# Gate visits merged, gate weights loaded into columns, two output tiles evicted in halves, and a new written order

## The chip, the cores and the metric

The kernel runs on one core of one Trainium2 chip. The metric is the device time of one execution in microseconds (us). The kernel before was timed three times: 266.11, 266.49 and 266.73, median 266.49.

## The reference, cut to what matters

The output is `g * a + (1 - g) * b` for 2048 tokens of 512 features in bf16. `a` is an attention with a memory over four segments of 512 tokens and 32 heads of 16 features; `b` is a GLU with 1792 hidden features; `g` is one gate for each token. Both branches read `A_x`.

```python
x = A_x
g = sigmoid((x * gate_w).sum(-1, keepdims=True))
q, k, v = x @ wq, x @ wk, x @ wv          # heads, 4 segments of 512
for s in range(4):
    logits = qs @ ks.T * 0.25 + mask      # keys after the query are masked
    a_dot = softmax(logits) @ vs
    a_mem = (phi(qs) @ M) / (phi(qs) @ z + 1e-6)
    o = gb * a_mem + (1 - gb) * a_dot     # gb = sigmoid(beta), one per head
    M = M + phi(ks).T @ vs;  z = z + sum(phi(ks))
a = o @ wo
b = (gelu(x @ w_gate) * (x @ w_up)) @ w_down
return g * a + (1 - g) * b
```

## The kernel before, in words

The program is a list of named tasks. A task is one or a few instructions on one engine. A long string `ORDER`, written out, lists all tasks; each engine runs its tasks in the order of that string, and a task that takes a new PSUM bank names it there behind a colon (`out3_1_0:0` takes bank 0). Four banks (`psD`) are shared by the dense matmuls, the weighted sums and the small products; one four-bank region (`psX`) takes the score fills, one at a time. Waits are derived from what tasks read and write, bank reuse included. So the string alone sets the order on each engine, and on SP's queue the order in which DMAs are issued; an instruction that waits holds up all behind it on its engine.

Names carry the segment first, then the tile. For segment `s`:

- `xtr0_n`, `xev0_n`: the first segment's x is loaded in four pieces (`ld_x0_hk`: token half h, feature half k), turned on TensorE by 16 transposes (L773) and copied out on VectorE or ScalarE (L781, L782). The x of later segments comes by DMA transposes `ld_xS_kb` (L331) into one of three buffers `xT`, so that segment 3 uses the buffer of segment 0.
- `K`, `Q`, `V`: projections in groups of four matmuls of 512 columns, emitted in pairs `a` and `b` (L452; the first two K tiles in halves of 256 columns, L477); `Kev`, `Qev`, `Vev` evict them on either engine, `kpada` and `kpadb` write masked copies of k (L488), and `phka`, `phkb`, `phkc` compute phi (L462 to L465; `phq...` for q).
- `vsh` (L503) are shifted copies of v, and `ktr` (L562) transposes of phi(k), both by DMA from SP.
- `mz` (L567): 64 small matmuls, the memory sums; `mzacc` adds them up on VectorE. `nz`, `nd`, `ndp`, with the transposes `tpS_z` and `tpS_m`, read the memory.
- `stS_tX` (L597): a fill of scores, t a quarter of the heads and X one of A to E; `exp` (L603) on ScalarE; `msk` (L609) on GpSimd; `pvS_t` (L640): 64 matmuls, the weighted sums, in eight blocks of keys, each waiting for its own mask; `tpS_dtj` (L520), `pvp` (L650, L651) and `ot` (L657 adds the memory part, L659 transposes into `oT`) follow on VectorE. `oT` is one buffer for all segments.
- `G`, `gelu` or `gd`, `U`, `h` (L689, VectorE): the two GLU products. `outS_q_p` (L702): the down product of output tile q in five pieces of 2 or 3 matmuls. `wev` (L707 on ScalarE, L710 on VectorE) scales it by 1 - g, called `omgt`; `wo` (L718) is the attention's output product; `oev` (L722, VectorE) adds `gtok` times it; `dma` (L725) stores the tile through one of two buffers `ost`. The last tile, 15, has `wo` and `oev` in two halves of 256 columns and two stores, from SP and ScalarE.
- `gate`, `gz`, `gr`, `go`: the token gates of one segment, each a visit of its own to a bank: 16 matmuls of one column of weights by 128 tokens (L421), a transpose and a clamp on VectorE (L428, L429), exp on ScalarE (L430), and `omgt`, `gtok` on VectorE (L432 to L434).

The gate weights are loaded by SP as four rows of 128 into a corner of `omem` (`ld_gw`), turned into four columns by a small matmul (`gwtr`, L744) and copied to `gatew` (`gwev`, L746). Large weights come in halves of 0.9 MB: `wg0`, `wg1`, `wu0`, `wu1`, `wd0`, `wd1`. The head of the string, where the loads and the start are laid out, reads:

```python
ld_wk10 ld_wq00 ld_wq01 ld_wq10 ld_wv ld_beta ld_gw ld_wg0 ld_wg1 ld_x1_2 ld_x1_1 ld_x1_0 ld_x1_3 xtr0_0:1 xtr0_1:2
xtr0_3:3 xtr0_2:0 xev0_3:a xev0_2:a causal vones0 xev0_0:d xev0_1:d K0_1a:1 K0_0a:2 K0_0b K0_1b K0_2a:3 K0_2b Kev0_2:d
```

Of the kernel before, what the change touches and what calls it, by code (L numbers as in the profile page):

```python
# [14 lines left out]
P = 128  # L15
# [220 lines left out]
def _build(es, nc, A_x, A_wq, A_wk, A_wv, A_wo, A_beta, B_w_gate, B_w_up, B_w_down, gate_w, out):  # L236
# [40 lines left out]
    gt = sb("gt", [P, P], F32)  # L277
# [31 lines left out]
    def bk(s):  # L309
        return ("bank", s)  # L310
# [12 lines left out]
    gw4, ball = omem[0:4, 0, 0:P], omem[:, 1, 0:H]  # L323
# [21 lines left out]
    ld_w("gw", SP, gw4, gate_w.rearrange("(kb p) -> kb p", p=P), [("gw4",)], 0.01, ["x0_10"])  # L345
# [68 lines left out]
    def gates(s):  # L414
        sl = Slot()
        c = slice(4 * s, 4 * s + 4)

        mm = []
        for kb in range(4):
            for i in range(4):  # L420
                mm.append(I(lambda e, i=i, kb=kb: e.matmul(  # L421
                    BK[sl.i][32 * i:32 * i + 1, 0:128], gatew[:, kb:kb + 1],
                    xT[s % R_XT][:, kb, :].rearrange("p (q j r) -> p j q r", j=4, r=32)[:, i],
                    start=(kb == 0), stop=(kb == 3), tile_position=(0, 32 * i)),
                    [*x_of(s % R_XT, kb), ("gatew",)], [bk(sl)]))
        one(f"gate{s}", PE, 0.26, mm)
        one(f"gz{s}", DVE, 0.36, [
            I(lambda e: e.transpose(gt[:, :], BK[sl.i][:, 0:128]), [bk(sl)], [("gt",)]),  # L428
            I(lambda e: e.tensor_scalar(gz[:, c], gt[:, 0:128:32], ZMAX, None, ALU.min), [("gt",)], [("gz", s)])])  # L429
        one(f"gr{s}", ACT, 0.2, [I(lambda e: e.activation(gr[:, c], gz[:, c], ACTF.Exp), [("gz", s)], [("gr", s)])])  # L430
        one(f"go{s}", DVE, 1.2, [
            I(lambda e: e.tensor_scalar(gr1[:, c], gr[:, c], 1.0, None, ALU.add), [("gr", s)], [("gr1", s)]),  # L432
            I(lambda e: e.reciprocal(omgt[:, c], gr1[:, c]), [("gr1", s)], [("omgt", s)]),
            I(lambda e: e.tensor_tensor(gtok[:, c], gr[:, c], omgt[:, c], ALU.mult), [("gr", s), ("omgt", s)],  # L434
              [("gtok", s)]),
        ])
# [32 lines left out]
    def project(s):  # L469
# [36 lines left out]
        gates(s)  # L506
# [50 lines left out]
    def memory_write(s):  # L557
# [3 lines left out]
        for t in range(4):  # L561
# [4 lines left out]
        sl = Slot()  # L566
        one(f"mz{s}", PE, 0.45, [I(lambda e, c=c, kt=kt, g=g, sl=sl: e.matmul(  # L567
# [10 lines left out]
                [("mzacc",), ("gphm",)], [("mzq",)])])  # L578
        one(f"zq{s}", POOL, 0.25, [I(lambda e: e.tensor_tensor(
# [112 lines left out]
    def outputs(s):  # L692
        for qt in range(4):
# [4 lines left out]
            for pi, (a, z) in enumerate(((0, 3), (3, 6), (6, 8), (8, 11), (11, 14))):  # L698
                mm = []
                for fb in range(a, z):  # L700
# [8 lines left out]
                    [bk(sl), ("omgt", s)], [("wds", wi)])]),  # L709
                (DVE, 0.66, [I(lambda e, sl=sl, gt=gt, wi=wi: e.tensor_scalar(  # L710
                    wds[wi][:, :], BK[sl.i][:, :], omgt[:, gt:gt + 1], None, ALU.mult),
                    [bk(sl), ("omgt", s)], [("wds", wi)])])], L_DVE)
            last = gt == 4 * NSEG - 1
            parts = (slice(0, 256), slice(256, 512)) if last else (slice(0, 512),)
            ko = [[("ost", oi, 0)], [("ost", oi, 1)]] if last else [[("ost", oi, 0), ("ost", oi, 1)]]
            for ci, c in enumerate(parts):
                so = Slot()
                one(f"wo{s}_{qt}_{ci}", PE, 4 * T_MM / len(parts), [I(lambda e, kb=kb, q=q, so=so, c=c: e.matmul(  # L718
                    BK[so.i][:, c], oT[:, kb, q], wo[:, kb, c], start=(kb == 0), stop=(kb == 3)),
                    [("oT", kb), ("wo", kb, 0), *([("wo", kb, 1)] if kb < 3 else [])], [bk(so)]) for kb in range(4)])  # L720
                one(f"oev{s}_{qt}_{ci}", DVE, 0.66 / len(parts) + 0.03, [I(
                    lambda e, so=so, gt=gt, wi=wi, oi=oi, c=c: e.scalar_tensor_tensor(  # L722
                        out=ost[oi][:, c], in0=BK[so.i][:, c], scalar=gtok[:, gt:gt + 1], in1=wds[wi][:, c],
                        op0=ALU.mult, op1=ALU.add), [bk(so), ("gtok", s), ("wds", wi)], ko[ci])])
                one(f"dma{gt}_{ci}", (SP, ACT)[ci], 0.5, [I(lambda e, gt=gt, oi=oi, c=c: e.dma_start(  # L725
                    out[0, gt * 128:(gt + 1) * 128, c], ost[oi][:, c]), ko[ci], [("out", gt, ci)],
                    dma_sem=sem(f"s_out{gt}_{ci}"))], lat=2.0)
                outs.append(f"s_out{gt}_{ci}")
# [3 lines left out]
    def head_gates():  # L732
# [3 lines left out]
        for c in range(4):  # L736
            for m0, m1, h in ((2 * c, 8, 8 * c), (0, 2 * c, 8 * c + 8 - 2 * c)):
                if m0 < m1:
# [4 lines left out]
        sg = Slot()  # L743
        one("gwtr", PE, T_TR, [I(lambda e: e.transpose(BKbf[sg.i][:, 0:4], gw4, ident[0:4, 0:4]),  # L744
                                 [("gw4",), ("omem", 0), ("ident",)], [bk(sg)])])
        one("gwev", DVE, 0.1, [I(lambda e: e.tensor_copy(gatew[:, :], BKbf[sg.i][:, 0:4]), [bk(sg)], [("gatew",)])])  # L746
# [39 lines left out]
    for s in range(NSEG):  # L786
        if s == NSEG - 1:
            ld_xt(s)
# [63 lines left out]
ld_wk10 ld_wq00 ld_wq01 ld_wq10 ld_wv ld_beta ld_gw ld_wg0 ld_wg1 ld_x1_2 ld_x1_1 ld_x1_0 ld_x1_3 xtr0_0:1 xtr0_1:2  # L852
xtr0_3:3 xtr0_2:0 xev0_3:a xev0_2:a causal vones0 xev0_0:d xev0_1:d K0_1a:1 K0_0a:2 K0_0b K0_1b K0_2a:3 K0_2b Kev0_2:d
Kev0_0:a Kev0_1:a kpadb0_1 phka0_0 K0_3a:0 K0_3b Q0_1a:2 Q0_0a:1 Q0_0b Kev0_3:a phkb0_0 kpada0_0 kpada0_1 phka0_2
kpada0_2 kpadb0_2 kpadb0_0 kpada0_3 kpadb0_3 Q0_2a:3 Q0_2b Qev0_0:a Qev0_2:a Q0_1b Qev0_1:a Q0_3a:0 Q0_3b Qev0_3:a
V0_2a:1 gwtr:3 V0_1a:2 gwev st0_0A:0 gate0:0 phkc0_0 gz0 V0_1b V0_0a:3 V0_0b V0_3a:0 V0_3b exp0_0A phkb0_2 st0_0B:0
exp0_0B Vev0_0:d Vev0_1:d Vev0_3:d V0_2b G0_2a:3 G0_3a:2 G0_3b G0_1a:0 st0_0C:0 Gev0_3:d betab G0_2b G0_1b G0_0a:2
G0_0b Vev0_2:a exp0_0C Q1_3a:1 Gev0_1:d Gev0_0:a st0_0D:0 V1_3a:0 V1_3b Q1_2a:2 Q1_2b Q1_3b phkc0_2 Vev1_3:d Qev1_2:d
Qev1_3:d exp0_0D bexp Gev0_2:a st0_0E:0 exp0_0E gr0 gate1:0 G0_6a:2 G0_6b K1_1a:3 V1_0a:1 K1_1b vsh0_20 vsh0_00
vsh0_01 vsh0_21 ld_wu1 Gev0_6:d Kev1_1:d gz1 st0_1A:0 exp0_1A G1_6a:2 V1_0b G1_6b msk0_0C msk0_0B msk0_0D msk0_0A  # L860
msk0_0E pv0_0:30 st0_1B:0 Gev1_6:a tp0_d00:0 Vev1_0:a exp0_1B G0_4a:2 G0_4b gq Gev0_4:d tp0_d01:1 pvp0_01 K1_3a:1
K1_3b Kev1_3:a K1_2a:3 st0_1C:0 exp0_1C Q1_1a:2 K1_0a:0 K1_0b G0_5a:1 G0_5b st0_1D:0 exp0_1D ld_wo00 ld_wo10 ld_wo30
ld_x2_1 ktr0_1 ktr0_3 ld_wo11 ktr0_2 ld_x2_2 ld_wo01 ld_wu0 ktr0_0 ld_wd0 ld_wo21 ld_x2_0 ld_x2_3 ld_wd1 Kev1_0:d
Gev0_5:d pvp0_00 Q1_1b G1_1a:0 K1_2b V1_1a:1 V1_1b Kev1_2:d ot0_0 Vev1_1:d Qev1_1:d st0_2A:0 exp0_2A msk0_1A msk0_1D
msk0_1C msk0_1B G0_10a:3 G1_1b G0_10b Gev1_1:d gph kpada1_3 go0 gd0_10 G1_13a:1 G1_13b G0_8a:2 G0_8b G1_7a:0 G1_7b
gd1_13 gd1_7 G0_13a:3 G0_13b gd0_13 gd0_8 G0_9a:1 G0_9b gd0_9 G1_9a:0 G1_9b gd1_9 gelu0 st0_2B:0 pv0_1:32 kpadb1_3
tp0_d11:2 tp0_d10:1 kpadb1_0 G0_7a:1 G0_12a:0 G0_12b gd0_12 G1_8a:2 G0_7b G0_11a:3 G0_11b gd0_7 gd0_11 G1_8b gd1_8
U0_4a:0 Q1_0a:1 U0_4b U0_9a:3 kpada1_2 pvp0_10 kpadb1_2 pvp0_11 h0_4 phka1_2 U0_9b U0_3a:2 h0_9 U0_3b U0_8a:0 Q1_0b
phka1_0 Qev1_0:d U0_8b h0_8 exp0_2B st0_2C:0 phkb1_2 exp0_2C mz0:3 U0_5a:1 U0_1a:0 U0_1b U0_5b st0_2D:0 h0_3 mzacc0
h0_1 h0_5 phqa1_0 G1_3a:2 U0_11a:3 V1_2a:0 U0_11b h0_11 V1_2b Vev1_2:d kpadb1_1 exp0_2D st0_2E:0 G1_3b U0_6a:1 G1_5a:3  # L870
G1_5b U0_6b exp0_2E Gev1_5:a phqa1_2 Gev1_3:d h0_6 phkc1_2 st0_3A:0 G1_2a:0 U0_7a:2 G1_2b msk0_2B msk0_2C msk0_2D
msk0_2A exp0_3A msk0_2E pv0_2:31 phqb1_0 Gev1_2:d tp0_d21:0 tp0_d20:1 st0_3B:0 U0_7b U0_12a:0 G1_4a:1 U0_12b G1_4b
h0_7 h0_12 exp0_3B st0_3C:0 exp0_3C U0_13a:3 G1_0a:2 U0_13b G1_0b U0_10a:0 st0_3D:0 pvp0_20 kpada1_0 Gev1_4:d h0_13
kpada1_1 Gev1_0:d U0_10b U0_2a:1 U0_0a:3 h0_10 U0_2b h0_2 U0_0b K2_1a:2 h0_0 phqb1_2 exp0_3D phkb1_0 st1_0A:0 K2_3a:0
K2_1b K2_3b msk0_3A msk0_3B msk0_3C msk0_3D exp1_0A pv0_3:13 phkc1_0 st1_0B:0 Kev2_1:a Kev2_3:a exp1_0B K2_2a:2 K2_2b
Kev2_2:a tp0_d30:2 tp0_d31:1 K2_0a:0 G1_11a:1 K2_0b ld_x3_3 ld_wo20 ktr1_2 vsh1_00 ktr1_0 ktr1_1 vsh1_20 vsh1_01
vsh1_21 ktr1_3 st1_0D:0 gr1 exp1_0D Q2_3a:3 Q2_3b out0_0_0:2 out0_0_1 st1_0E:0 Qev2_3:d pvp0_21 Kev2_0:a exp1_0E
V2_3a:3 out0_1_0:0 V2_3b out0_1_1 Vev2_3:a st1_0C:0 exp1_0C msk1_0E zq0 msk1_0B msk1_0C msk1_0D msk1_0A out0_0_2
out0_1_2 G1_11b out0_1_3 out0_1_4 out0_0_3 ot0_1 pvp0_30 phqc1_0 pvp0_31 ot0_2 out0_0_4 Q2_1a:3 st1_1A:0 Q2_1b ot0_3
wev0_0:d wev0_1:d wo0_1_0:2 out0_3_0:0 out0_3_1 out0_3_2 Qev2_1:d kpada2_1 oev0_1_0 phqc1_2 out0_3_3 out0_3_4 pv1_0:32  # L880
tp1_d01:0 tp1_d00:2 gd1_11 gelu1 exp1_1A st1_1B:0 exp1_1B out0_2_0:1 out0_2_1 wo0_0_0:2 st1_1C:0 out0_2_2 G2_4a:3
# [77 lines left out]
```

## Time and profile before

| what | value |
|---|---|
| three timed runs | 266.11, 266.49, 266.73 us |
| profiled execution, first to last instruction (its span) | 266.5 us |
| what lies around the span | nothing that the times show: the span is the median |
| TensorE matmuls | 2816, busy 261.3 us |
| VectorE, ScalarE, GpSimd busy | 204.8, 207.2, 96.2 us |
| granted TensorE clock (mean) | 1.000 |
| DMA | 14.92 MB, 56 GB/s in the mean |

Busy time of TensorE counts overlapping matmuls once, and the ends of matmuls are modelled; what one matmul costs is read from start to start. LDWEIGHTS run beside the matmuls. A wait is put down to the semaphore that came last.

### The profile page before, as it was taken

The page shows a single profiled execution, that of the slowest core. Times are in us where ns is not written, and L with a number is a line of the kernel's source. Part 1 is how long each engine was busy: PE and PEld are TensorE (multiplying, and loading weights), DVE is VectorE, ACT ScalarE, POOL GpSimd, SP SyncE. Part 2 cuts the span into 40 slices and gives each one's busy share as a digit, 9 for nine tenths or more (in the row PEclk, how much of TensorE's full clock was granted, in tenths as well). Part 3 has the DMA queues.
Part 4 walks back from the last instruction along what each step waited for, and adds up shares of the span by engine and source line. Part 5 has one row for each costly group of instructions (what it writes and reads, how often), then busy time and mean ns, then how long its engine had stood idle before and what let it go on. Part 6 is the DMA issues. An engine that isn't in the chain of part 4 may idle for free.

```text
span 266.5 us, 6614 instructions
## 1 busy us (share of the span) xinstructions
PE 261.3 (98%) x2816; PEld 112.4 (42%) x2816; DVE 204.8 (77%) x389; ACT 207.2 (78%) x170; POOL 96.2 (36%) x160
## 2 busy tenths in 40 slices
PE   6999999999999999999999999999999999999995
PEld 2634444443443443444444443444344444434442
DVE  1466578578976669998797998897987797968975
ACT  1589888988899988989988979749798967477601
POOL 6003705036430816042254538423635035072600
PEclk9999999999999999999999999999999999999999
DMA  6993339950025120000004100011001000010002
GB/s 195 264 214 53 149 75 156 235 158 0 2 48 109 23 59 22 2 0 4 20 2 64 39 2 2 20 42 39 4 15 52 2 0 2 2 59 2 20 2 79
DMA packets 25251, 14.92 MB, mean 56 GB/s; under 512 B 14086, under 2 KB 24198, under 8 KB 25222
## 3 DMA queue, kind: packets, MB, share of 16 engines
q1 hardware_dynamic: 23990, 13.91, 22.3%
q10 hardware_dynamic: 1232, 0.59, 0.8%
q8 instruction: 22, 0.36, 0.5%
q14 instruction: 7, 0.06, 0.1%
HBM read 8.14 MB, written 2.10 MB: 38 GB/s over the span
## 4 chain that ended last, share of the span: by engine, by line
PE 97%; DMA 2%; issue 0%; DVE 0%; SPq 0%; DVEq 0%
PE psD L452 54%; PE psD L702 19%; PE psX L597 9%; PE psD L640 7%; PE psD L718 5%; DMA pt<-in_A_x_dram 2%; PE psD L477 1%; PE psD L773 1%; PE psD L567 1%; PE psD L421 0%; PE psX L545 0%; PE psD L535 0%; DVE ost L722 0%; SPq L327 0%; DVEq L806 0%
## 5 line engine op out<-in xcount | busy, mean ns | idle before, releaser
L603 ACT ACTIVATE pt<-psX 128x2048 bf16<-128x2048 f32 x72 | 135.1, 1876 | 32.3 <-PE psX L597 31.6
L609 POOL TENSOR_TENSOR pt<-pt,ctri 128x256 bf16<-128x256 bf16 x128 | 90.9, 717 | 153.9 <-ACT pt L603 149.4
L452 PE MATMUL psD<-xT,wu 128*128 128x512 bf16 x224 | 58.0, 380 | 0.0
L452 PE MATMUL psD<-xT,wg 128*128 128x512 bf16 x224 | 56.4, 380 | 0.0
L702 PE MATMUL psD<-wd,gb 128*128 128x512 bf16 x224 | 54.4, 380 | 0.0
L689 DVE TENSOR_TENSOR gb<-psD,gb 128x512 bf16<-128x512 f32 x56 | 37.5, 683 | 11.9 <-PE psD L452 11.5
L520 DVE STREAM_TRANSPOSE tT<-psD 128x512 f32<-128x512 f32 x35 | 23.4, 695 | 11.3 <-PE psD L640 11.1
L702 PEld LDWEIGHTS psD<-wd,gb 128*128 128x128 bf16 x224 | 20.7, 98 | 25.8 <-issue 2.8
L452 PEld LDWEIGHTS psD<-xT,wg 128*128 128x128 bf16 x224 | 20.3, 98 | 26.2 <-issue 2.8
L452 PEld LDWEIGHTS psD<-xT,wu 128*128 128x128 bf16 x224 | 20.1, 98 | 25.6 <-issue 3.7
L597 PE MATMUL psX<-qT,kD 32*128 32x192 bf16 (+7 forms) x512 | 28.6, 287 | 0.0
L597 PEld LDWEIGHTS psX<-qT,kD 32*128 32x128 bf16 x512 | 8.2, 92 | 25.9 <-ACT pt L603 19.5
L651 DVE SCALAR_TENSOR_TENSOR ob<-tT,gq,rc 128x256 bf16<-128x256 f32 x32 | 18.2, 570 | 1.1
L640 PE MATMUL psD<-pt,vnat 64*17 64x128 bf16 (+7 forms) x512 | 18.7, 283 | 0.0
L445 DVE CAST gb<-psD 128x512 bf16<-128x512 f32 x23 | 15.7, 684 | 3.7 <-PE psD L452 3.6
L640 PE MATMUL psD<-pt,vsh 64*17 64x128 bf16 (+7 forms) x512 | 18.3, 283 | 0.0
L452 PE MATMUL psD<-wv,xT 128*128 128x512 bf16 x64 | 18.0, 381 | 0.0
L452 PE MATMUL psD<-xT,wq 128*128 128x512 bf16 x64 | 17.0, 380 | 0.0
L718 PE MATMUL psD<-wo,oT 128*128 128x512 bf16 (+1 forms) x68 | 16.2, 367 | 0.0
L640 PEld LDWEIGHTS psD<-pt,vnat 64*17 64x17 bf16 x512 | 11.6, 86 | 8.7 <-issue 3.8
L680 ACT ACTIVATE gb<-psD 128x512 bf16<-128x512 f32 x28 | 14.7, 602 | 0.3 <-PE psD L452 0.3
L452 PE MATMUL psD<-xT,wk 128*128 128x512 bf16 x56 | 14.6, 380 | 0.0
(96 smaller groups left out, 250.4 us busy)
## 6 DMA issues: line engine op xcount, KB each, us to landing
out_dram<-ost SPq DMA_DIRECT2D x15, 128.0 KB, 1.7
wg<-in_B_w_gate_dram SPq DMA_DIRECT2D x2, 896.0 KB, 6.9
wu<-in_B_w_up_dram SPq DMA_DIRECT2D x2, 896.0 KB, 5.4
wd<-in_B_w_down_dram SPq DMA_DIRECT2D x2, 896.0 KB, 7.3
vsh<-vnat SPq DMA_DIRECT2D x16, 68.0 KB, 2.1
wq<-in_A_wq_dram SPq DMA_DIRECT2D x4, 128.0 KB, 4.8
wv<-in_A_wv_dram SPq DMA_DIRECT2D x1, 512.0 KB, 4.7
pt<-in_A_x_dram SPq DMA_DIRECT2D x2, 128.0 KB, 3.5
```

Of the source, the lines that this page charges most:

```text
L445: (DVE, 0.60, [I(lambda e: e.tensor_copy(dst, src()), [bk(sl), *reads], writes)]),
L452: one(f"{name}{'abcd'[h // 2]}", PE, 2 * T_MM, [I(lambda e, i=i: e.matmul(BK[sl.i][:, :], lhs(i), rhs(i), start=(i == 0), stop=(i == n - 1 ...
L520: one(f"tp{name}", DVE, 0.605, [I(lambda e, ts=ts, bank=bank: e.transpose(tT[ts.i][:, :], bank()), [key], [("tT", ts)])])
L597: ins.append(I(lambda e, c=c, kb=kb, ncol=ncol, c0=c0, g=g: e.matmul(XALL[:, g * 512 + c0:g * 512 + c0 + ncol], kD[b][quad(g), c, kb, :], ...
L603: one(f"exp{s}_{name}", ACT, 2048 * 0.000833 + 0.05, [I(lambda e: e.activation(pt[slot][:, :, :], xin, ACTF.Exp, scale=ATT_SCALE), [("X", ...
L609: ins.append(I(lambda e, mv=mv: e.tensor_tensor(mv, mv, cm, ALU.mult), [("pt", slot), ("causal",)], [("pt", slot)]))
L640: ins.append(I(lambda e, kb=kb, slot=slot, c0=c0, n=n, g=g, c=c, r0=r0, sl=banks[j], va=va: e.matmul(BK[sl.i][32 * c:32 * c + 17, 64 * kb: ...
L651: I(lambda e, ts=ts, t=t, j=j, dst=dst: e.scalar_tensor_tensor(out=dst, in0=t_rows(ts, 16), scalar=gq[:, 2 * t + j:2 * t + j + 1], in1=rc_ ...
L680: one(f"gd{s}_{ft}", ACT, 0.485, [I(lambda e, gi=gi, f=f, sl=sl: e.activation(gb[gi][:, f, :], BK[sl.i][:, :], ACTF.Gelu_apprx_tanh), [bk( ...
L689: one(f"h{s}_{ft}", DVE, 0.605, [I(lambda e, sl=sl, gi=gi, f=f: e.tensor_tensor(gb[gi][:, f, :], BK[sl.i][:, :], gb[gi][:, f, :], ALU.mult ...
L702: mm.append(I(lambda e, fb=fb, gi=gi, f=f, q=q, sl=sl: e.matmul(BK[sl.i][:, :], gb[gi][:, f, q], wd[:, fb, :], start=(fb == 0), stop=(fb = ...
L718: one(f"wo{s}_{qt}_{ci}", PE, 4 * T_MM / len(parts), [I(lambda e, kb=kb, q=q, so=so, c=c: e.matmul(BK[so.i][:, c], oT[:, kb, q], wo[:, kb, ...
```

## The change

Five things change.

1. The gates of segments 0 and 1, and of 2 and 3, are computed together: 32 matmuls into the upper half (columns 256 to 511) of the bank that the memory sums `mz0` and `mz1` use, just ahead of them. `gz`, `gr` and `go` then run once for two segments, on twice the columns.
2. The gate weights are loaded by one DMA straight into four columns of `gatew`; `gwtr` and `gwev` go.
3. Tile 14 has `wo` and `oev` in halves like tile 15, but is still stored by one DMA, from SP.
4. The loads of segment 3's x are declared with segment 1 instead of segment 3.
5. The whole string `ORDER` is written anew.

The core of the diff:

```diff
-    ld_w("gw", SP, gw4, gate_w.rearrange("(kb p) -> kb p", p=P), [("gw4",)], 0.01, ["x0_10"])
+    load("gw", SP, lambda e: e.dma_start(gatew[:, :], gate_w.rearrange("(kb p) -> p kb", p=P),
+                                         allow_slow_non_contiguous=True), [("gatew",)], wait=[("ld", "x0_10")])
...
+    def gate_products(h, sl):
+        one(f"gate{h}", PE, 0.5, [I(lambda e, i=i, kb=kb, s=s: e.matmul(
+            BK[sl.i][32 * i:32 * i + 1, 256 + 128 * (s % 2):384 + 128 * (s % 2)], gatew[:, kb:kb + 1],
+            xT[s % R_XT][:, kb, :].rearrange("p (q j r) -> p j q r", j=4, r=32)[:, i],
+            start=(kb == 0), stop=(kb == 3), tile_position=(0, 32 * i)),
+            [*x_of(s % R_XT, kb), ("ld", "gw")], [bk(sl)])
+            for s in (2 * h, 2 * h + 1) for kb in range(4) for i in range(4)])
+
+    def gates(h, sl):
+        c = slice(8 * h, 8 * h + 8)
+        one(f"gz{h}", DVE, 0.5, [
+            I(lambda e: e.transpose(gt[:, :], BK[sl.i][:, 256:512]), [bk(sl)], [("gt",)]),
+            I(lambda e: e.tensor_scalar(gz[:, c], gt[:, 0:256:32], ZMAX, None, ALU.min), [("gt",)], [("gz", h)])])
...
         sl = Slot()
+        if s < 2:
+            gate_products(s, sl)
         one(f"mz{s}", PE, 0.45, [I(lambda e, c=c, kt=kt, g=g, sl=sl: e.matmul(
...
+        if s < 2:
+            gates(s, sl)
...
+            split = gt >= 4 * NSEG - 2
             last = gt == 4 * NSEG - 1
-            parts = (slice(0, 256), slice(256, 512)) if last else (slice(0, 512),)
+            parts = (slice(0, 256), slice(256, 512)) if split else (slice(0, 512),)
...
+                if last or ci == len(parts) - 1:
+                    kd, d = (ko[ci], c) if last else ([k for kk in ko for k in kk], slice(0, 512))
+                    one(f"dma{gt}_{ci}", (SP, ACT)[last and ci], 0.5, [I(lambda e, gt=gt, oi=oi, d=d: e.dma_start(
...
-        one("gwtr", PE, T_TR, [I(lambda e: e.transpose(BKbf[sg.i][:, 0:4], gw4, ident[0:4, 0:4]),
-                                 [("gw4",), ("omem", 0), ("ident",)], [bk(sg)])])
-        one("gwev", DVE, 0.1, [I(lambda e: e.tensor_copy(gatew[:, :], BKbf[sg.i][:, 0:4]), [bk(sg)], [("gatew",)])])
...
-        if s == NSEG - 1:
-            ld_xt(s)
+        if s == 1:
+            ld_xt(3)
```

Of the new order, the start (TensorE's tasks and SP's loads), one stretch with the second gate visit, and the end:

```python
ld_wk10 ld_wq00 ld_wq01 ld_wq10 ld_wv ld_beta ld_wg0 ld_gw ld_x1_2 ld_wg1 ld_x1_0 xtr0_2:0 xtr0_0:1 xtr0_1:2 xtr0_3:3
xev0_3:a vones0 xev0_0:d xev0_1:d K0_1a:1 xev0_2:a K0_0a:2 K0_1b K0_2a:3 K0_2b causal K0_0b Kev0_2:d Kev0_1:a kpadb0_1
...
oev0_2_0 pvp1_10 Gev2_6:a gate1:2 h1_0 kpadb2_0 mz1 V2_0a:0 V2_0b G2_13a:1 msk1_2A gelu2 gz1 U1_3a:3 Vev2_0:d U1_3b
...
U3_9a:1 ot3_0 st3_3C:0 exp3_3C h3_4 oev2_3_0 U3_9b out3_0_0:3 h3_9 out3_0_1 out3_0_2 st3_3D:0 out3_0_3 out3_0_4
out3_1_1 pvp3_20 exp3_3D ot3_1 out3_1_2 dma10_0 msk3_3A msk3_3B wev3_0:a msk3_3C pvp3_21 ot3_2 out3_1_3 msk3_3D
pv3_3:31 out3_2_0:2 tp3_d31:2 tp3_d30:0 out3_2_1 pvp3_31 out3_1_4 out3_2_2 pvp3_30 out3_3_0:1 out3_3_1 dma11_0
wev3_1:a ot3_3 wo3_1_0:0 wo3_0_0:3 out3_2_3 out3_3_2 oev3_0_0 out3_2_4 oev3_1_0 out3_3_3 out3_3_4 wev3_2:d wo3_2_0:3
wev3_3:a dma12_0 wo3_2_1:2 wo3_3_0:0 oev3_2_0 dma13_0 oev3_2_1 dma14_1 oev3_3_0 wo3_3_1:3 dma15_0 oev3_3_1 dma15_1
```

In the old string the end reads:

```python
msk3_2A msk3_2C msk3_2D msk3_2E pv3_2:21 h3_7 h3_4 tp3_d21:1 tp3_d20:0 pvp3_11 exp3_3A st3_3B:0 wo2_3_0:3 out3_1_0:0
...
U3_9a:1 exp3_3B st3_3C:0 U3_9b out3_0_0:2 out3_0_1 out3_0_2 exp3_3C st3_3D:0 exp3_3D msk3_3B msk3_3A msk3_3C msk3_3D
oev2_3_0 ot3_0 h3_9 pvp3_20 pvp3_21 ot3_1 ot3_2 out3_0_3 out3_1_1 out3_1_2 out3_0_4 out3_1_3 out3_1_4 pv3_3:31
tp3_d31:2 tp3_d30:0 pvp3_31 pvp3_30 ot3_3 wev3_1:d wev3_0:a dma10_0 dma11_0 out3_2_0:2 out3_2_1 out3_3_0:1 out3_2_2
out3_2_3 out3_2_4 out3_3_1 wo3_0_0:3 wo3_1_0:0 out3_3_2 oev3_0_0 oev3_1_0 dma12_0 dma13_0 out3_3_3 out3_3_4 wo3_2_0:3
wev3_2:a wev3_3:d wo3_3_0:0 wo3_3_1:2 oev3_2_0 oev3_3_0 oev3_3_1 dma14_0 dma15_0 dma15_1
```

SP's loads after `wv` and `beta` come in this order before: `gw`, `wg0`, `wg1`, `x1_2`, `x1_1`, `x1_0`, `x1_3`, four `vsh0`, `wu1`; afterwards: `wg0`, `gw`, `x1_2`, `wg1`, `x1_0`, `x1_1`, `wu1`, `x1_3`, three `vsh0`. On TensorE, `Q1_3a` comes four pairs of G matmuls behind `st0_0C` before, and directly behind it afterwards. `wd1` moves from behind the x2 loads to behind `ktr1_1`.

## The prediction

> **What bounds the kernel now.** I read the page's busy shares first, then the chain that ended last, then TensorE's own waits, and then the order of time at the two ends.
>
> ```profile
> PE 261.3 (98%) x2816; PEld 112.4 (42%) x2816; DVE 204.8 (77%) x389; ACT 207.2 (78%) x170; POOL 96.2 (36%) x160
> ...
> PE 97%; DMA 2%; issue 0%; DVE 0%; SPq 0%; DVEq 0%
> ```
>
> 97% of the chain is TensorE. Its own waits (the waits view for PE alone) are two, both in the first 6 us:
>
> ```profile
> PE psD L773 <- DMA pt<-in_A_x_dram: 1.4, 1, 1.4
> PE psD L369 <- POOL warm L365: 1.1, 1, 1.1
> ```
>
> From 5.65 to about 263.7 us TensorE never stands. So the time is the first useful matmul, plus the sum of TensorE's slots (start of one group to start of the next), plus the tail behind the last matmul. An edit counts only if it takes a slot away, moves an end, or opens a hole. One stretch of the timeline gives the prices:
>
> ```profile
> 15.11 0.59 PE L452 MATMUL psD<-wv,xT 128*128 128x512 bf16 x2
> 15.63 0.17 PE L744 MATMUL psD<-ident,omem 4*128 4x4 bf16 x1
> 15.74 0.61 PE L452 MATMUL psD<-wv,xT 128*128 128x512 bf16 x2
> 16.28 0.40 PE L597 MATMUL psX<-qT,kD 32*128 32x512 bf16 x4
> 16.60 0.39 PE L421 MATMUL psD<-xT,gatew 128*1 128x128 bf16 x16
> 16.93 2.33 PE L452 MATMUL psD<-wv,xT 128*128 128x512 bf16 x10
> ```
>
> A dense 512-column matmul takes 0.216. From dense into a group of another shape costs 0.10 more (15.11 to 15.63 is 0.53 for two). A score fill or a gate visit takes 0.33 in all, of which a gate visit is four rounds of 0.055 and 0.11 of leaving. The two timed ends are 266.11 and 266.73, the median 266.49, and the profiled span 266.5; so nothing measurable lies around the span and the sum is made against 266.5. A measurement of this kernel can tell about 0.2%, 0.53 us, from no change.
>
> **Gates.** The four visits take 0.326, 0.326, 0.342 and 0.327, together 1.32. Afterwards there are two visits of eight rounds, 2 x 0.44 = 0.88, directly followed by the memory sums. Before, mz1 directly followed by gate2 has a slot of 0.536, while mz0 and mz2, followed by dense work, have 0.639 and 0.597; so these two shapes change over without the 0.10, and mz1 gets its leaving cost back (+0.10). Saved: 1.32 - 0.88 - 0.10 = 0.34. If the change-over costs 0.10 after all, 0.14; if mz1 pays nothing, 0.44. The VectorE and ScalarE work of the gates (ten VectorE instructions fewer) is hidden: no slot waits for it, and omgt is first read by the output stage, some 15 us later.
>
> **Gate weights.** The transpose at L744 goes: 0.10 into it and 0.105 for it, 0.20 saved, with a VectorE copy of 0.16 beside it. The load becomes 512 elements of 2 bytes. The nearest row is the beta load, 128 runs of 64 bytes, which landed 0.19 after the wv load ahead of it in the queue; four times that is 0.8, and 0 is the other end; I take 0.3. Nobody waits for gatew until gate0, near 56 us. What it delays is queued behind it on SP: the x1 transposes.
> [...]
>
> **Head.** What is loaded first decides the start.
>
> ```profile
> 1.07 3.17 PE L369 MATMUL psD<-warm 128*128 128x512 bf16 x7 [1.07 <-POOL warm L365]
> 5.65 1.89 PE L773 MATMUL psD<-ident,pt 128*128 128x128 bf16 x16 [1.41 <-DMA pt<-in_A_x_dram]
> 7.33 2.76 PE L477 MATMUL psD<-xT,wk 128*128 128x256 bf16 x16
> 9.93 1.89 PE L452 MATMUL psD<-xT,wk 128*128 128x512 bf16 x8
> ```
>
> TensorE starts with xtr0_0, whose data (x0_00) landed at 5.60 in the trace's landing records; x0_10 landed at 3.44. Afterwards xtr0_2, on x0_10, comes first: it fills 4.03 to 4.46, and only three transposes of 0.427 stand behind 5.65. K0 starts at 6.93, not 7.33. But in the trace 256-column matmuls come every 0.213 until 9.04 and every 0.109 from there. If that step stays at 9.06, the 0.43 gained is slow time worth half, 0.21. Ends: 0.43 if the step moves along, 0 if an eviction intervenes. Walking VectorE and ScalarE through the new order (evictions 0.61 to 0.69, masked key copies 0.26 start to start) brings Qev0_2, the last input of the first fill, to 15.8; TensorE needs it at 16.3.
>
> **x1 and the SP queue.** Q1_3b now wants x1_3 at 22.4 (before, its first reader is V1_3b at 25.1), and the queue ahead of x1_3 has become wg0, gw, x1_2, wg1, x1_0, x1_1, wu1. In the trace wg0 and wg1 together took 6.0 from wv's landing and an x1 transpose 0.5. Three weights, four transposes and gw: 10.6 + 9.0 + 2.0 + 0.3 = 21.9; with the 2.5 that wd1 took behind a transpose, 20.4. I take no wait; the margin is the rival below. wd1, moved from 50.9 to behind ktr1_1 at about 79.4, lands at 84.2 by wu1's 4.8; out0_1_2 needs it at 86.1. The x3 loads move ahead of the second segment's vsh copies, and wait for xT[0] to be read out at 74.5; the copies are wanted at 95.
>
> **VectorE's queue.** ot (L657, L659) overwrites oT and so waits for the previous segment's last wo. The new order puts ot3_0 ahead of h3_4, and wo2_3_0 behind out3_1_0. From the start of st3_3B: wo2_3_0 ends at 1.84, seen 0.2 later; transpose 0.71 and h3_4 0.68 less 0.08 overlap give 3.36; out3_0_0, which reuses h3_4's bank, would start at 3.13. A hole of 0.29, bounds 0 to 0.5. Behind ot3_0 stand h3_4, oev2_3_0 and h3_9. The same sum for ot1_1 ahead of h1_8 (K3_1a waits) gives 0.15, for ot2_1 ahead of h2_2 (pv2_3) 0.05; as sums this fine err by 0.1, I take 0.10 for the two.
>
> **Tail.**
>
> ```profile
> 254.29 1.31 DVE L520 STREAM_TRANSPOSE tT<-psD 128x512 f32<-128x512 f32 x2 [1.32 <-PE psD L640]
> ...
> 257.44 0.71 DVE L659 STREAM_TRANSPOSE oT<-ob 128x512 bf16<-128x512 bf16 x1
> ...
> 258.40 1.89 PE L718 MATMUL psD<-wo,oT 128*128 128x512 bf16 x8
> ...
> 262.92 1.53 DVE L722 SCALAR_TENSOR_TENSOR ost<-psD,gtok,wds 128x512 bf16<-128x512 f32 x3
> 264.48 0.36 ACTq L725 DMA_DIRECT2D out_dram<-ost  x1
> ```
>
> pv3_3 ends at 254.07; VectorE has oT at 258.15, 4.08 later, and 20 dense matmuls (4.32) cover that. The new order has 17 there (3.67), so wo3_1_0 waits 0.46. Behind it on TensorE stands everything to the end. Against that, four half evictions replace one whole and two halves: from the start of wo3_2 the last one ends at 2.42 (last matmul issued 1.75, 0.20 to be seen, 0.47) instead of 2.60. Together +0.46 - 0.18 = +0.28; pv3_3 coming three matmuls earlier is only moved work. The output of tile 14 still leaves whole, after both halves.
> pv3_3 also follows its last fill by 3.45 instead of 4.10. The masks are done 3.88 after the fill, and pv reads that block 0.57 in, so 0.15 remains: no hole. It also waits for wev3_0 on ScalarE now (bank 3), done 2.9 after the fill. The other short distances (3.87) have more. Between two fills the new order keeps at least 2.37 on TensorE, as the old one did (fill to exp 0.45, exp 1.88, 0.055 to be seen).
>
> **Sum.** -0.34 - 0.20 - 0.21 + 0.28 + 0.29 + 0.10 = -0.08; all other slots are the same tasks, with as many entries from dense work. 266.4, with 266.0 to 267.0 as this case's own range.
>
> **Rivals.** *The holes do not open* (0.27): VectorE runs ahead of my sums and the head's 0.43 counts whole: -0.34 - 0.20 - 0.43 + 0.28 = -0.69, 265.8; without the tail's wait 265.4. For: the trace before has no hole, so the order was laid out with care. Against: ot's wait for wo is a fact of the new order.
> *The clock steps earlier* (0.05): xtr0_2 makes the stretch before 5.65 busier (from 4.03 it ran to 4.46 of it). If full speed came at 5.65, three transposes of 0.22 would end at 6.3, VectorE's copies at 6.9, and K0_1b, which needs ScalarE's second copy at about 7.7, at 8.3 instead of 9.3: 265.4. The step before is 3.41 after 5.65. [...]
> *x1_3 comes late* (0.28): in the trace its first part landed at 18.82 and its last at 20.50, 1.7 later. Such a straggler on the 21.9 gives 23.6, 1.2 past Q1_3b's need at 22.4, and TensorE stands for all of it: 267.6; with half of it 267.0 to 267.2. It decides once x1_3 lands after 22.4. Against it: wd1's faster row.
> *It does not do what it says*: no shared change-over costs +0.20 and stays within no change; it is in the first case.
>
> **Numbers.** The likeliest, 0.40: 266.4. Faster 0.32, slower 0.28. From 265.3 to 267.6 the range holds the rivals' prices and leaves out later stragglers and several gains at once.
>
> **What would show it.** Two gate slots of 0.44 just ahead of the memory sums, and no transpose of the gate weights. K0 at 6.9. No wait of PE on the xT transposes near 22; if there is one, the third rival. Holes of 0.3 at out3_0_0 (about 246) and of 0.5 ahead of the first wo behind the last weighted sum. The forecast is wrong in kind if PE's waits sum to over 1.5 us behind 6 us, or if the L477 matmuls run fast from the start.

## The result and the profile after

The changed kernel takes 268.55 us (median of four runs, 267.97 to 269.37), the kernel before 266.42 beside it: ratio 1.0077, 95% interval 1.0064 to 1.0091. It is slower by 2.1 us. The forecast was 266.4, with a range up to 267.6.

The page of the changed kernel, its busy line and its chain:

```profile
PE 256.1 (96%) x2782; PEld 112.3 (42%) x2819; DVE 203.0 (76%) x379; ACT 207.4 (78%) x168; POOL 96.4 (36%) x160
...
PE 80%; DVE 7%; DMA 6%; issue 3%; SPq 2%; ACT 0%; ACTq 0%
```

The chain was 97% TensorE; now VectorE and DMA have 13% of it. (37 of the 2819 matmul records are missing in this profile, which leaves seeming gaps called "issue"; the profile of c_after below has all records and no such gap among TensorE's waits.) The waits view for TensorE alone, columns: line and who released it, sum, number, longest in us:

```profile
PE psD L450 <- DMA xT<-in_A_x_dram: 1.1, 1, 1.1
...
PE psD L450 <- DVE gb L690: 0.4, 1, 0.4
...
PE psD L641 <- DVE vnat L443: 0.3, 1, 0.3
PE psX L598 <- DVE kD L486: 0.3, 1, 0.3
```

Before, both waits lay in the first 6 us. Now one on x1 and several behind VectorE lie in the middle. Slot by slot (start of a group to start of the next, minus the same slot in a gapless run) the holes are: 1.32 at Q1_3b, where x1_3 landed at 22.29 and TensorE stood ready for it at 21.0; and six behind VectorE, at 40 us (0.20, G1_13a waits for Vev1_1), 75.6 (0.33, st1_0A for kpada1_0), 76.2 (0.28, K2_3a for h0_10, next in VectorE's queue), 142.9 (0.41, pv1_3 for Vev2_1), 156 (0.30 inside pv2_0, h2_7) and 195 (0.27 inside pv2_3, h2_2). The six make 1.8. The timeline at the second and third of them (start, duration, engine, line, in brackets the idle time before and its releaser; the first matmul of K2_3a, at 76.23, is among the missing records, so that its row shows 0.43 and not 0.28):

```profile
74.75 1.42 POOL L610 TENSOR_TENSOR pt<-pt,ctri 128x256 bf16<-128x256 bf16 x2 [0.71 <-ACT pt L604]
...
74.79 0.78 DVE L486 TENSOR_SCALAR kD<-kT,maskA 128x512 bf16<-128x512 bf16 x1
...
75.63 0.39 PE L598 MATMUL psX<-qT,kD 32*128 32x512 bf16 x4 [0.27 <-DVE kD L486]
...
76.46 0.38 PE L450 MATMUL psD<-xT,wk 128*128 128x512 bf16 x1 [0.43 <-DVE gb L690]
```

The masked key copy kpada1_0 (L486) takes 0.78 here, and 0.35 where nothing disturbs it. It began 0.04 behind a GpSimd mask. The view shows no wait for it: the time appears as its own duration. TensorE's wait behind it does show.

Two things went as planned. The gate visits take 0.44 each, directly ahead of the memory sums, as a second execution of the changed kernel (c_after below) shows without a missing record:

```profile
55.63 0.62 PE L416 MATMUL psD<-xT,gatew 128*1 128x128 bf16 x32
...
56.07 0.71 PE L566 MATMUL psD<-vnat,phkt 128*32 128x34 bf16 x64
...
56.72 0.60 PE L450 MATMUL psD<-xT,wu 128*128 128x512 bf16 x2
```

And from the start of TensorE's last group (`wo3_3_1`) to the end of the span it is 3.21 us, against 3.38 in the profile before.

### The profile page after: what moved, and what is told of

It reads as the page before. It is cut to its first block, busy times and chain, and to the rows that moved or that the text cites. A ratio compares the mean times of both kernels' runs of the same rounds, so it can differ in the third digit from the quotient of the medians.

```text
span 267.6 us, 6577 instructions
## 1 busy us (share of the span) xinstructions
PE 256.1 (96%) x2782; PEld 112.3 (42%) x2819; DVE 203.0 (76%) x379; ACT 207.4 (78%) x168; POOL 96.4 (36%) x160
## 4 chain that ended last, share of the span: by engine, by line
PE 80%; DVE 7%; DMA 6%; issue 3%; SPq 2%; ACT 0%; ACTq 0%
PE psD L450 43%; PE psD L703 17%; PE psX L598 7%; PE psD L641 6%; PE psD L720 5%; DMA xT<-in_A_x_dram 2%; DMA wv<-in_A_wv_dram 2%; SPq L331 1%; DMA pt<-in_A_x_dram 1%; DVE gb L690 1%; DVE ob L652 1%; DVE kD L486 1%; DVE tT L517 1%; PE psD L566 1%; DVE ost L724 1%
## 5 line engine op out<-in xcount | busy, mean ns | idle before, releaser
L450 PE MATMUL psD<-xT,wu 128*128 128x512 bf16 x213 | 54.6, 379 | 1.8 <-issue 1.8
L450 PE MATMUL psD<-xT,wg 128*128 128x512 bf16 x216 | 54.3, 380 | 1.0 <-issue 0.8
L703 PE MATMUL psD<-wd,gb 128*128 128x512 bf16 x214 | 52.5, 380 | 1.5 <-issue 1.3
L703 PEld LDWEIGHTS psD<-wd,gb 128*128 128x128 bf16 x224 | 20.1, 98 | 25.9 <-issue 3.8
L724 DVE SCALAR_TENSOR_TENSOR ost<-psD,gtok,wds 128x512 bf16<-128x512 f32 (+1 forms) x18 | 12.1, 683 | 9.3 <-PE psD L720 9.3
L641 PE MATMUL psD<-pt,vsh 64*17 64x320 bf16 (+7 forms) x512 | 18.2, 283 | 0.0
L652 DVE SCALAR_TENSOR_TENSOR ob<-tT,gq,rc 128x256 bf16<-128x256 f32 x32 | 16.6, 520 | 1.1
L450 PE MATMUL psD<-wv,xT 128*128 128x512 bf16 x62 | 16.9, 380 | 0.3 <-issue 0.3
L443 DVE CAST gb<-psD 128x512 bf16<-128x512 f32 x20 | 13.4, 682 | 3.4 <-PE psD L450 3.3
```

Source lines behind the costliest of these rows:

```text
L450: one(f"{name}{'abcd'[h // 2]}", PE, 2 * T_MM, [I(lambda e, i=i: e.matmul(BK[sl.i][:, :], lhs(i), rhs(i), start=(i == 0), stop=(i == n - 1 ...
L641: ins.append(I(lambda e, kb=kb, slot=slot, c0=c0, n=n, g=g, c=c, r0=r0, sl=banks[j], va=va: e.matmul(BK[sl.i][32 * c:32 * c + 17, 64 * kb: ...
L652: I(lambda e, ts=ts, t=t, j=j, dst=dst: e.scalar_tensor_tensor(out=dst, in0=t_rows(ts, 16), scalar=gq[:, 2 * t + j:2 * t + j + 1], in1=rc_ ...
L703: mm.append(I(lambda e, fb=fb, gi=gi, f=f, q=q, sl=sl: e.matmul(BK[sl.i][:, :], gb[gi][:, f, q], wd[:, fb, :], start=(fb == 0), stop=(fb = ...
```

## Experiments

Ratios are to the kernel before, run beside the kernel on the same chip. VectorE's copies have line L486 in the changed kernel and those made from it, L488 in the kernel before.

**c_before, the kernel before again.**

> The kernel before once more, unchanged, as a control. Theory A: the profile before (span 266.5) caught an execution whose second piece of x, x0_00, landed late (5.60 against 4.77 in the profile after), and some 1.75 us lie around the span in every execution, as they do in the four executions of the changed kernel (269.37 against a span of 267.6, and three more with the same difference); then the spans of ordinary executions here are about 264.7 and the times 266.4. Rival: the span is the time, as the prediction said; then the spans are about 266.4.

266.44 (266.14 to 266.66), ratio 1.000 (0.9991 to 1.0009); the profiled execution took 266.56 with a span of 264.8, and in all ten the time is 1.7 to 1.8 above the span. Theory A. So the profile the prediction was made on (span 266.5) was not a usual execution: x0_00 landed at 5.60 there and at 4.69 here, and TensorE's 256-column matmuls ran at 0.109 from 6.9 on instead of 9.04. Two errors of 1.7 us, that execution and "nothing lies around the span", had cancelled. Apart from the first 10 us the two traces agree slot by slot.

**e_head, only the transposes' order.**

```diff
-xtr0_0:1 xtr0_1:2 xtr0_3:3 xtr0_2:0 xev0_3:a xev0_2:a
+xtr0_2:0 xtr0_0:1 xtr0_1:2 xtr0_3:3 xev0_2:a xev0_3:a
```

> The kernel before with the group of transposes xtr0_2 (and its eviction) put ahead of the others, and nothing else changed. Theory A (the head term of the prediction): K0 starts 0.4 earlier and half of that stays, 266.2; with the clock stepping up early, as at 5.84 in the profile after, up to 1.0 less, 265.4. Rival B: the clock steps up where it did, and a wait behind the head (an eviction, x1) takes the rest: 266.4.

266.52, ratio 0.9995 (0.9981 to 1.0009): nothing. That is nearest to rival B's number, but neither theory names the wait that the timeline shows:

```profile
4.03 1.91 PE L773 MATMUL psD<-ident,pt 128*128 128x128 bf16 x16
...
6.38 0.38 PE L477 MATMUL psD<-xT,wk 128*128 128x256 bf16 x2 [0.43 <-DMA wk<-in_A_wk_dram]
```

The transposes start earlier, and K0 then waits for the key weights: wk00 landed at 6.25 and K0 starts at 6.38. In the control they are 6.16 and 6.29, in the profile after 6.36 and 6.49. What starts the useful work here is wk00, not x; only in the profile of the prediction, with its late x0_00, does K0 start later than that (wk00 at 6.50, K0 at 7.33).

**e_x13, x1_3 ahead of wu1 in the changed kernel.**

```diff
-ld_wu1 ... ld_x1_3
+ld_x1_3 ld_wu1
```

> The changed kernel with one load moved: x1_3 is issued ahead of wu1 and not behind it. x1_3 should land near 19.9 and not 22.29. Theory A (the wait of 1.3 us at Q1_3b is lost time): 267.2 to 267.4. Rival B (TensorE then only runs into VectorE's queue, whose later holes at 40, 76, 143, 157 and 196 us grow by what is gained): 268.2 to 268.6.

268.14 (267.67 to 268.30), ratio 1.0060 (1.0047 to 1.0072). x1_3 lands at 19.05, TensorE does not stand at Q1_3b, and the median falls by 0.41 only. In the profiled executions the wait was 1.32 (the slowest of four) and 1.16 (c_after below), so the median gain is smaller than the hole that a profile shows. (The profiled execution of e_x13 is the fastest of its five, 267.67; what makes the other four longer is not shown.) The six holes stay as they were: 0.21, 0.33, 0.28, 0.42, 0.30, 0.27. Neither theory's number; the larger part of the loss lies behind VectorE.

**e_dve and e_dve2, only VectorE's order.** e_dve is e_x13 with six instructions moved:

```diff
-Kev1_0:d st0_1D:0 exp0_1D Q1_1b kpada1_3
+st0_1D:0 exp0_1D Q1_1b kpada1_3 Kev1_0:d
-pvp0_20 go0
+go0 pvp0_20
```

and likewise h1_11 to behind pvp1_21, h1_10 to behind phqc2_2, ot2_1 to behind h2_2, and h3_4 to behind pvp3_11.

> The run e_x13 with six instructions moved in VectorE's own order (Kev1_0, pvp0_20, h1_11, h1_10 and ot2_1 later, h3_4 earlier), TensorE's order and the edits unchanged. Theory A (the six holes of 0.21, 0.33, 0.28, 0.42, 0.30 and 0.27 in the trace of e_x13, together 1.8, come from what stands ahead in VectorE's queue): 266.3 to 266.6. Rival B (VectorE has too much to do, the holes only move on): 267.8 to 268.2.

266.81 (266.71 to 267.38), ratio 1.0014 (1.0005 to 1.0023): 1.3 of the 1.67 above the kernel before are gone, with TensorE's order unchanged. That is theory A, 0.2 above its range. Four holes are closed, and two are new, 0.14 at 157 us and 0.07 at 42; the pair at 74 us (0.33 and 0.28) is unchanged, since kpada1_0 met a mask again:

```profile
73.15 1.42 POOL L610 TENSOR_TENSOR pt<-pt,ctri 128x256 bf16<-128x256 bf16 x2 [0.73 <-ACT pt L604]
...
73.16 0.81 DVE L486 TENSOR_SCALAR kD<-kT,maskA 128x512 bf16<-128x512 bf16 x1
```

e_dve2 moves that one copy:

```diff
-pvp0_21 ... kpada1_0
+kpada1_0 pvp0_21
```

> e_dve with one instruction moved: kpada1_0 stands one place earlier in VectorE's order, ahead of the pair pvp0_21. In the trace of e_dve it began at 73.16, 0.01 behind a GpSimd mask, and took 0.81; GpSimd stood idle from 72.41 to 73.15. Theory A (the copy stands still while a mask runs): it now starts near 72.5, takes 0.35, the holes of 0.33 and 0.28 at 74 us go, and the time is 266.2. Rival B (the copy's time is its own, or the queue's length counts): it takes 0.8 again, and the time stays 266.8.

```profile
72.49 0.34 DVE L486 TENSOR_SCALAR kD<-kT,maskA 128x512 bf16<-128x512 bf16 x1
...
73.15 1.64 POOL L610 TENSOR_TENSOR pt<-pt,ctri 128x256 bf16<-128x256 bf16 x2 [0.74 <-ACT pt L604]
```

The same copy, in the gap of GpSimd, takes 0.34. The hole of 0.33 is gone, the one of 0.28 is 0.14, and the profiled span is 264.6 instead of 265.1. GpSimd now has the delay: its first mask here meets pvp0_21 and takes 0.89 instead of 0.67, and nobody waits for it. So the trace shows what theory A says of this copy (0.81 begun 0.01 behind a mask, 0.34 clear of one). The median does not show its price: 266.68 (266.05 to 268.37), ratio 0.9999 (0.9981 to 1.0018), with 266.2 expected.

**e_mask and c_mask, GpSimd's masks cut.** The edit, in e_x13 and in the kernel before:

```diff
-cm = bass.AP(causal, 0, [[64, P], [0, 4], [1, 64]])
+cm = bass.AP(causal, 0, [[64, P], [0, 4], [1, 8]])
-mv = pt[slot][:, :, c0:c0 + 64]
+mv = pt[slot][:, :, c0:c0 + 8]
```

> The run e_x13 with GpSimd's mask instructions cut to 8 of their 64 columns; seven eighths of the mask is left out, and nothing is changed in order. Theory A (VectorE's copies from SBUF to SBUF stand still while GpSimd works, kpad 0.35 alone and 0.64 to 0.84 beside a mask, and that is what makes VectorE late): all kpad near 0.35, no hole over 0.1 behind VectorE, 266.3 or a little less. Rival B (VectorE is late by its order and the sum of its own work alone): the holes stay, 268.0 to 268.2.

> The kernel before with GpSimd's mask instructions cut to 8 of their 64 columns, as a control for e_mask; seven eighths of the mask is left out. The trace before shows TensorE without a hole, so by every theory nothing is to be gained: 266.3 to 266.5. If it is faster by over 0.3, the cut itself shortens TensorE's path and e_mask has to be read against it.

e_mask: 265.97 (265.67 to 266.28), ratio 0.9981 (0.9972 to 0.9990). c_mask: 266.46, ratio 1.0002 (0.9993 to 1.0011). The groups of e_mask (count, busy sum in us, mean ns):

```profile
L610 POOL TENSOR_TENSOR pt<-pt,ctri 128x32 bf16<-128x32 bf16 x128 | 33.9, 269 | 201.5 <-ACT pt L604 197.1
...
L486 DVE TENSOR_SCALAR kD<-kT,maskB 128x512 bf16<-128x512 bf16 x16 | 5.3, 339 | 0.0
L486 DVE TENSOR_SCALAR kD<-kT,maskA 128x512 bf16<-128x512 bf16 x16 | 5.3, 338 | 0.0
```

and of the changed kernel:

```profile
L610 POOL TENSOR_TENSOR pt<-pt,ctri 128x256 bf16<-128x256 bf16 x128 | 91.2, 716 | 149.7 <-ACT pt L604 145.2
...
L486 DVE TENSOR_SCALAR kD<-kT,maskA 128x512 bf16<-128x512 bf16 x16 | 7.5, 473 | 0.0
L486 DVE TENSOR_SCALAR kD<-kT,maskB 128x512 bf16<-128x512 bf16 x16 | 6.4, 406 | 0.0
```

Without the long masks each key copy takes 0.34, no hole over 0.1 is left behind VectorE, and the same order is 2.17 faster (268.14 - 265.97; the two ran on different chips, with the kernel before at 266.47 on both). VectorE's busy time falls from 202.6 to 193.9: some 9 us of it was standing, about a third of that on key copies. In the kernel before the same cut also takes 8.9 us off VectorE (204.7 to 195.8), and gains nothing: there the copies that stood were not waited for. So the gain of e_mask does not come from the cut as such. Theory A, and c_mask as expected.

The traces of c_after and e_mask, which have the same order on TensorE, also tie each hole to an instruction. Just ahead of each, in VectorE's order, stands one that took longer in c_after than in e_mask: kpada1_3 (0.66 and 0.34) at 40 us, go0, kpadb1_0 and kpada1_0 (together 2.96 and 1.34) at 75 and 76, phqa2_0 (0.89 and 0.47) at 143, phqc2_2 (1.59 and 1.22) at 156, pvp2_20 (0.97 and 0.76) at 195. The fourth of them in the profile after, with the eviction behind it and TensorE's wait for that:

```profile
141.24 0.89 DVE L460 TENSOR_SCALAR phq<-qT 128x1024 bf16<-128x1024 bf16 x1
...
142.06 0.68 DVE L443 CAST vnat<-psD 128x512 bf16<-128x512 f32 x1
...
142.88 0.39 PE L641 MATMUL psD<-pt,vnat 64*17 64x512 bf16 x4 [0.35 <-DVE vnat L443]
```

**e_oldorder2 and e_oldorder3, the edits in the old order.** The tasks taken out stood scattered over the string; gr1 and go1 stand behind gelu2 and gd2_12 in e_oldorder2, and behind exp2_2B and ahead of oev1_2_0 in e_oldorder3.

```diff
-gwtr:3 gwev gate0:0 gz0 gr0 go0 gate1:0 gz1 gr1 go1 gate2:1 gz2 gr2 go2 gate3:0 gz3 gr3 go3
-mz0:3 ... mz1:2
+gate0:3 mz0 ... mzacc0 gz0 ... msk0_2E gr0 ... h0_13 go0 ... gate1:2 mz1 ... mzacc1 gz1
-wo3_2_0:3 wev3_2:a wev3_3:d wo3_3_0:0 wo3_3_1:2 oev3_2_0 oev3_3_0 oev3_3_1 dma14_0 dma15_0 dma15_1
+wev3_2:d wo3_2_0:3 wev3_3:a wo3_2_1:2 wo3_3_0:0 oev3_2_0 oev3_2_1 dma14_1 oev3_3_0 wo3_3_1:3 dma15_0 oev3_3_1 dma15_1
```

> The four edits of the change with the order written before, adapted only where the edits force it (gates ahead of mz0 and mz1, the end of the string as in the new order). Theory A (the new order costs what was lost, the edits themselves gain): the slots gwtr -0.20, gates -0.30, the end -0.18 leave 265.7. Rival B (an edit costs: the column load, the longer visits): 268 or more. Rival C (TensorE arrives earlier at evictions and exps that are not earlier, and waits there): 266.2 to 266.5.

268.73, ratio 1.0083 (1.0069 to 1.0097), which looks like Rival B and is not:

```profile
122.84 1.28 ACT L428 ACT_TABLE_LOAD   x1
...
124.14 0.21 ACT L428 ACTIVATE gr<-gz 128x8 f32<-128x8 f32 x1
...
124.36 1.28 ACT L681 ACT_TABLE_LOAD   x1
...
125.66 2.06 ACT L681 ACTIVATE gb<-psD 128x512 bf16<-128x512 f32 x4
...
126.31 1.04 PE L720 MATMUL psD<-wo,oT 128*128 128x512 bf16 x4 [1.81 <-ACT gb L681]
```

One exp of 0.21 between two gelus costs two table loads (the rows ACT_TABLE_LOAD), 2.56 us of ScalarE, and TensorE waits behind them.

> e_oldorder2 with the ScalarE step gr1 and the VectorE step go1 moved behind the second segment's gelu group, to where the old order had gr3 and go3. In the trace of e_oldorder2 gr1 (an exp) stood between two gelus and brought two more table loads of 1.28 us on ScalarE (13 and not 11), and TensorE waited 1.88, 0.66 and 0.19 behind them. Theory A (that alone made e_oldorder2 slow, and the edits gain): 268.73 - 2.7 = 266.0, and 265.8 if all of the slots are kept. Rival B (an edit costs): 266.5 or more.

266.12 (265.95 to 266.39), ratio 0.9981 (0.9967 to 0.9995): 2.6 less, theory A. The edits themselves gain 0.39, and this version is faster than both kernels. Of the 0.69 that its slots give (gates 0.31, gwtr 0.20, end 0.18) 0.20 is lost again where st1_3C waits for exp1_3B, and 0.10 at G0_6a.

**e_best and c_after.** e_best is e_x13 with many moves, planned from measured durations with GpSimd's delays counted in; some three fifths of VectorE's tasks and four fifths of TensorE's keep their relative order, so no diff is shown.

> The four edits, x1_3 ahead of wu1, and an order in which VectorE's copies of q, k and of the weighted sums were moved to where no GpSimd mask is running, or to where nobody waits for them; TensorE's order is changed in places too, for instance so that fewer groups wait for a bank. Theory A (what is left of the loss is VectorE standing behind masks): TensorE has no hole over 0.15 after 10 us, and the time is at least as low as that of e_mask, 265.6 to 266.0. Rival B (the edits gain no more than the 0.4 of e_oldorder3 in any order): 266.1 or more.

268.30 (268.19 to 270.21), ratio 1.0067 (1.0042 to 1.0092): theory A falls for this order. TensorE has holes behind VectorE, of 0.49 at 80.7, 0.41 in pv2_3, 0.29 at 79.3 and 0.22 in pv3_1. Ahead of them stand again instructions that took longer than in e_mask: phkc1_0 (1.67 and 1.22) and go0 (0.83 and 0.65) ahead of the first and third, pvp2_20 (1.22 and 0.76) and ndp3_2 (0.97 and 0.65) ahead of the other two. So the planned order did not keep VectorE clear of the masks.

> The changed kernel once more, unchanged, as a control beside e_best on one chip. Theory A (x1_3 lands late by what its queue holds, differently in each execution): 268.0 to 269.4 as before, with Q1_3b waiting between 0.3 and 1.3. Rival B (the wait of 1.3 belonged to one execution): 268.1, as e_x13, without a wait there.

268.65 (268.09 to 269.15), ratio 1.0065 (1.0041 to 1.0090); Q1_3b waits 1.16, x1_3 landing at 21.86, and the six holes are there to 0.01. Theory A.

## Why the prediction was wrong

Two things make the kernel slow, VectorE standing behind masks and the late x1_3, and the edits themselves gain a little. Slot by slot, c_after's profiled execution is 2.9 us longer than e_mask's, which has the same order on TensorE: 1.16 at Q1_3b and 1.8 in the six holes, while the rest cancels. The medians split it otherwise: 2.17 for VectorE (e_x13 to e_mask) and 0.41 for x1_3 (changed kernel to e_x13). How much belongs to each is therefore known only to some 0.4 to 0.8. The edits gain 0.39 in the old order (e_oldorder3), and e_mask lies 0.50 under the kernel before. With -0.39, the medians add up to +2.19; measured are 268.55 - 266.42 = 2.13.

**The step that failed: "VectorE's queue".** It walked three places, all behind ot, gave 0.29 at out3_0_0 and 0.10 for the other two, and the sum then took "all other slots" as unchanged. Measured: 0.06 at out3_0_0, nothing at K3_1a, 0.27 in pv2_3 (forecast 0.05), and five holes that it does not name, 1.5 together. What it had wrong is the length of VectorE's instructions: it put none of them at more than it takes alone (the key copies, under "Head", at "0.26 start to start"). The groups of the profile before hide this in a mean:

```profile
L488 DVE TENSOR_SCALAR kD<-kT,maskB 128x512 bf16<-128x512 bf16 x16 | 6.9, 438 | 0.0
L488 DVE TENSOR_SCALAR kD<-kT,maskA 128x512 bf16<-128x512 bf16 x16 | 6.9, 434 | 1.2 <-ACT kT L444 1.2
```

Of these 32 copies 24 took 0.31 to 0.37, and eight 0.49 to 0.84. The new order puts such a copy, or another of VectorE's instructions that stand, ahead of one for which TensorE waits, at a time when a mask runs. The forecast's own sign, "wrong in kind if PE's waits sum to over 1.5 us behind 6 us", came true: the holes sum to 3.1 (1.32 and 1.8).

The traces show how long such an instruction stands. In the profile after twelve key copies met a mask, and each of them ended 0.15 after a mask's end (150 or 149 ns); in e_x13 eleven of twelve did, and one ended 0.20 after it. Masks take longer too, 0.66 to 1.63 in that profile: the 21 that started while one of VectorE's instructions of phi or the product in pvp (L460, L463, L652) ran, 0.18 or more before its end, ended 0.52 to 0.53 after that end. The prediction never weighed this.

**x1.** The landing was right in size (21.9 forecast, 22.29 measured; gw took 0.28 of the queue, forecast 0.3). The need was wrong: 22.4 came from the profile with the late start, and TensorE was there at 21.0. So the third rival's mechanism happened, and its point of decision was off by 1.4. The wait was 1.32 and 1.16 in the two profiles, near the rival's 1.2; its price was 0.4 in the median.

**Head.** -0.21 was worth nothing: K0 waits for wk00 (e_head). The step in pace at 9.04 (a 256-column matmul from 0.213 to 0.109), on which this term and a rival were built, was that one execution's; in each of the other profiles 256-column matmuls ran at 0.109 from 6.9 at the latest. The granted clock of that execution reads 1.00 both from 5.65 to 9.06 and from 9.06 to 16.30; that the step was one of the clock, and that a busier stretch ahead would bring it earlier, was the author's guess, and no run shows it.

**Base.** The sum was made against a span of 266.5 as if it were the time. A usual span is 264.7, and 1.75 lies around it. That the base was right all the same is luck.

**Tail.** The halves gave -0.18, as forecast. The wait of 0.46 ahead of wo3_1_0 (by the prediction's own 4.08 and 3.67 it is 0.41) did not come, and the row shows the slip:

```profile
258.04 0.71 DVE L660 STREAM_TRANSPOSE oT<-ob 128x512 bf16<-128x512 bf16 x1
...
258.35 1.89 PE L720 MATMUL psD<-wo,oT 128*128 128x512 bf16 x8
```

wo3_1_0 starts 0.40 before the transpose ends at 258.75; only its fourth matmul, at 259.00, reads that part of oT. The wait has to be set against the matmul that reads, 0.65 later, and not against the group.

**Right:** gates (forecast -0.34; visits 1.32 to 0.89, the two memory sums' slots 1.17 to 1.29, together -0.31), gwtr -0.20, and wd1 (landed at 85.87, needed at 87.15). The column load of 512 elements landed 0.28 behind the load ahead of it (wg0 at 14.70, gw at 14.98).

## What to carry to other kernels

Before an order is walked by durations, look at the spread of each group and not only at its mean: a copy that takes 0.35 at one place and 0.8 at another may be standing behind another engine, and no wait is shown for it. Put copies that TensorE needs soon into gaps of GpSimd (in e_dve2 one such move brought a copy from 0.81 to 0.34 and closed its hole, while a whole order planned that way, e_best, met masks at other places), and keep exps out of a run of gelus (in e_oldorder2 one of 0.21 brought two table loads of 1.28). And look at a second execution of the kernel before: one profile with a late landing shifts every deadline in it, here by 1.7 us.

## What the runs showed of the hardware

- GpSimd's 128 masks cost VectorE some 9 us of standing (202.6 to 193.9 busy in e_mask, 204.7 to 195.8 in c_mask), booked as busy time.
- The 56 products h, which read PSUM, did not stand: they took 0.65 to 0.69 in e_x13, beside masks and clear of them, and 0.65 to 0.69 in e_mask. In the profile after the 39 that met a mask and the 17 that met none took 0.65 to 0.69 as well.
- A table load on ScalarE takes 1.283 us; in e_oldorder2 the exp follows 0.02 after the load's end, and the pair of loads cost the kernel 2.6 (268.73 against 266.12).
- K0's first matmul starts 0.13 behind the landing of wk00: 6.25 and 6.38 in e_head, 6.16 and 6.29 in c_before, 6.36 and 6.49 in the profile after.
